# Attention scores of one head and 128 tokens in row halves of TensorE, with q and k transposed on TensorE in float32

## The chip, the cores and the metric

The kernel runs on one core of one Trainium2 chip. The metric is device microseconds of one execution, the median of several; lower is better. Engines are called PE (TensorE matmul), PEld (TensorE weight load), DVE (VectorE), ACT (ScalarE), POOL (GpSimd) and SP (SyncE, which issues most DMAs).

## The reference

Three layers follow each other. The first is causal attention with a decay bias over 4 batches, 8 heads, 576 tokens, head size 64; its rows (2304 x 512) go through a mixture of 8 experts with one expert per token, and then through a dense two-layer net.

```python
scores = scale * np.matmul(q, k.transpose(0, 1, 3, 2))
cum = np.cumsum(np.maximum(s, 0.0), axis=-1)
bias = -(cum[:, :, :, None] - cum[:, :, None, :])
scores = np.where(causal, -1000000000.0, scores + np.minimum(bias, 0.0))
attn = np.exp(scores - np.max(scores, axis=-1, keepdims=True))
attn = attn / (np.sum(attn, axis=-1, keepdims=True) + 1e-09)
x = np.matmul(attn, v)                      # to rows of 8 * 64 = 512
...
ye = np.maximum(xe @ w1[e], 0.0) @ w2[e]    # one expert e per token, gated
...
g = h * np.clip(h + 3.0, 0.0, 6.0) / 6.0    # h = x @ w_in
out = g @ w_out
```

## The kernel before

Every float32 product is made of float16 halves: x = hi + lo, and a product is hi*hi + hi*lo + lo*hi. The change touches the attention stage alone, and the experts and the dense net follow it in program order on the same engines.

Tokens of a batch are cut into blocks i = 0 to 4 of 128 rows (the last has 64), and a block with a pair p of heads is one `Pair`. There are 80 of them: 64 with 128 rows ("full") and 16 with 64 rows ("short"). Block i attends to W = 128 * (i + 1) keys (the short one to 576). For each pair the program writes these steps: `S`, the scores into PSUM (PE); `A`, add the decay sum `cp`, take the minimum and negate (DVE); `E`, the exponential (ACT); `T`, transposes of the weights in float32 (PE, L588); `CD`, the split of the transposed weights into `hi` (ACT, L610) and `lo` (DVE, L611); `V`, the product with v into `o` (PE, L644). `finish` divides by the row sum (DVE, L655 to L657). The steps of neighbouring pairs are interleaved in one loop over slots n: `T` of pair n-1, `S` of pair n+1, `A` and `E` of pair n, `V` of pair n-2. A scheduler of the recording layer then settles each engine's order, and engines execute strictly in that order.

In `S` of the kernel before, rows of the score tile are 64 tokens of each of the two heads, for tokens of one parity r. One matmul of 128 rows times 64 columns (L545) gives hi*hi + hi*lo for one head from a doubled k; one of 64 times 64 (L550) gives lo*hi; a 128 x 128 one adds the causal mask (L556). PSUM holds three score banks (`psS`), two for `o` (`psO`) and three for transposes (`psT`).

q and k come as float32 with tokens in rows. `prep` splits them into halves in row form (POOL L406, L467, L481; for the first 512 tokens of batch 0 on ACT and DVE, L457 to L461), and DMA transposes issued by SP (L440) turn them into `qT` and `kT`. The decay sums are computed for all heads at once, written to DRAM (`cum_d`, L394) and read back by broadcast into `cp` (L401), one head in each half of the partitions. v is loaded by DMA, scaled on ACT (L491), rounded on ACT (L492), and its rest is taken on POOL (L493). When the pieces of `prep` are issued is set by planned times (`at_time`, with a `lag` ahead of their use).

## Time and profile before

| quantity | value |
|---|---|
| median of 3 runs | 906.51 us (905.99 to 907.49) |
| the profiled execution's own time | 901.45 us |
| its span, first to last instruction | 899.8 us |
| mean granted TensorE clock | 0.967 |
| first expert matmul starts (end of attention) | 282.87 us |
| PE busy over the span | 834.1 us (93%) |

The profile shows one execution of the program. A duration of a matmul in it includes the way through the array, so the time that a stream of matmuls takes is read from start to start. "Idle before" an instruction is time in which its engine stood still, put down to what released it.

### The profile page before, as it was taken

The numbers are of one execution on the slowest core, as the hardware profiler recorded it, in microseconds if no ns is written. First come the engines' busy times: TensorE is split into PE (matmuls) and PEld (weight loads), VectorE is DVE, ScalarE is ACT, GpSimd is POOL, SyncE is SP. The second block draws the span as 40 slices with busy tenths as digits, with TensorE's granted clock in tenths as the row PEclk, the third lists the DMA queues.
The fourth block names the chain that finished last, engine by engine and source line by source line (L and its number), as shares of the span: only waits on it lengthen the run. The fifth ranks groups of instructions, "written<-read, shape, count | busy, mean of one in ns | idle before, by whom it ended". The sixth has DMA issues, their size and how long they took to land. (4 is left out here: it accounts for less than half of the span.)

```text
span 899.8 us, 17411 instructions
## 1 busy us (share of the span) xinstructions
PE 834.1 (93%) x6676; PEld 510.6 (57%) x6676; DVE 487.4 (54%) x1250; ACT 428.4 (48%) x831; POOL 260.9 (29%) x357
## 2 busy tenths in 40 slices
PE   2899899989989989899999999999999999999993
PEld 1466565667648987566777744444444444466441
DVE  5477774686856644977869489970351044013000
ACT  3587774699744343665546276640351044023000
POOL 3187869488742212232332100001000100000100
PEclk9999996699979999999999999999999999999997
DMA  8999999943125496988877213310000000000000
GB/s 182 177 209 191 200 211 168 197 147 121 31 55 111 144 210 190 278 308 266 261 217 265 71 48 105 107 48 35 12 1 12 24 12 0 24 24 1 24 36 14
DMA packets 147633, 106.61 MB, mean 118 GB/s; under 512 B 106838, under 2 KB 123478, under 8 KB 147542
## 3 DMA queue, kind: packets, MB, share of 16 engines
q1 hardware_dynamic: 143750, 95.36, 42.0%
q0 software_dynamic: 3792, 10.06, 3.5%
q8 instruction: 54, 0.88, 0.4%
q14 instruction: 37, 0.30, 0.1%
HBM read 78.65 MB, written 9.66 MB: 98 GB/s over the span
## 5 line engine op out<-in xcount | busy, mean ns | idle before, releaser
L1219 PE MATMUL ph<-x2T,wi 128*128 128x512 f16 (+1 forms) x960 | 187.4, 358 | 0.0
L1093 PE MATMUL py<-wo,gT 128*128 128x512 f16 x864 | 187.1, 379 | 0.0
L1219 PEld LDWEIGHTS <-wi 128*128 128x128 f16 x960 | 94.0, 98 | 92.8
L1093 PEld LDWEIGHTS <-gT 128*128 128x128 f16 x864 | 84.5, 98 | 101.7
L1225 DVE SCALAR_TENSOR_TENSOR t<-t,ph 128x512 f32<-128x512 f32 (+1 forms) x80 | 50.5, 632 | 141.3 <-ACT t L1224 141.2
L1260 POOL DMA_INDIRECT out_dram<-o,orows x18 | 17.6, 977 | 355.7 <-ACT o L1258 346.3
L1081 PE MATMUL ph<-xsT,t 128*128 128x224 f16 (+7 forms) x960 | 110.0, 276 | 8.2 <-DVE hT L1086 7.0
L1193 PE MATMUL py<-hT,t 128*128 128x224 f16 (+7 forms) x960 | 109.2, 273 | 6.3 <-DVE hT L1086 5.9
L1081 PEld LDWEIGHTS <-t 128*128 128x128 f16 x960 | 86.9, 100 | 28.9 <-issue 9.1
L1193 PEld LDWEIGHTS <-t 128*128 128x128 f16 x960 | 85.4, 98 | 28.6 <-issue 9.0
L1258 ACT ACTIVATE o<-py 128x512 f32<-128x512 f32 x18 | 10.7, 597 | 163.5 <-PE py L1093 163.5
L611 DVE SCALAR_TENSOR_TENSOR lo<-pt,hi 128x256 f16<-128x256 f32 (+3 forms) x144 | 72.6, 521 | 27.8 <-ACT hi L610 27.0
L610 ACT ACTIVATE hi<-pt 128x256 f16<-128x256 f32 (+3 forms) x144 | 63.8, 461 | 42.3 <-PE pt L588 41.3
L257 DVE SCALAR_TENSOR_TENSOR t<-wf,t 128x1024 f16<-128x1024 f32 x53 | 64.6, 1222 | 34.8 <-ACT t L254 34.5
L575 ACT ACTIVATE pp<-ne,nm 128x128 f32<-128x128 f32 (+4 forms) x144 | 76.9, 581 | 13.2 <-DVE nm L569 13.2
L588 PE MATMUL pt<-idf,pp 128*128 128x128 f32 (+1 forms) x400 | 74.6, 306 | 5.1 <-ACT pp L575 2.6
L569 DVE CUSTOM_DVE_ANT_0 ne<-sp,cp 128x128 f32<-128x128 f32 (+4 forms) x144 | 61.5, 456 | 29.7 <-ACT pp L575 10.9
L254 ACT ACTIVATE t<-wf 128x1024 f16<-128x1024 f32 x53 | 55.6, 1055 | 43.7 <-DMA wf<-in_moe_w_dram 43.4
L1226 ACT ACTIVATE gT<-t 128x512 f16<-128x512 f32 (+1 forms) x80 | 46.9, 586 | 49.8 <-DVE t L1225 49.8
L644 PE MATMUL o<-v,hi 128*128 128x65 f16 (+2 forms) x960 | 64.6, 204 | 5.8 <-ACT hi L610 5.4
L1227 DVE SCALAR_TENSOR_TENSOR gT<-t,gT 128x512 f16<-128x512 f32 (+1 forms) x80 | 51.0, 638 | 31.3 <-ACT gT L1226 29.7
L1224 ACT ACTIVATE t<-ph,three 128x512 f32<-128x512 f32 (+1 forms) x80 | 51.3, 642 | 32.0 <-PE ph L1219 32.0
(170 smaller groups left out, 1097.4 us busy)
## 6 DMA issues: line engine op xcount, KB each, us to landing
wf<-in_moe_w_dram SPq DMA_DIRECT2D x64, 512.0 KB, 6.0
wd<-in_moe_w_in_dram SPq DMA_DIRECT2D x16, 512.0 KB, 5.4
wd<-in_moe_w_out_dram SPq DMA_DIRECT2D x16, 512.0 KB, 3.7
v<-in_v_dram SPq DMA_DIRECT2D x36, 128.0 KB, 4.4
k<-in_k_dram SPq DMA_DIRECT2D x8, 512.0 KB, 5.1
q<-in_q_dram SPq DMA_DIRECT2D x8, 512.0 KB, 5.9
x_d<-xw SPq DMA_DIRECT2D x16, 256.0 KB, 3.3
cp<-cum_d SPq DMA_DIRECT2D x6, 576.0 KB, 7.4
```

Source lines behind the costliest of these rows:

```text
L254: nc.scalar.activation(hi, fv, AF.Copy, scale=sc)
L257: stt(out=lo, in0=fv, scalar=sc, in1=hi, op0=ALU.mult, op1=ALU.subtract)
L569: mark["dve"] = nc.vector.tensor_tensor_reduce(out=ne[:, a:z], in0=sp, in1=c[:, a:z], op0=ALU.add, op1=ALU.min, scale=-1.0 / SC, scalar=se ...
L575: mark["act"] = nc.scalar.activation(self.view(self.pp, e), self.view(self.ne, e), AF.Exp, bias=self.nm[:, e:e + 1], scale=-1.0).ins
L588: nc.tensor.transpose(dst, src, idf)
L610: nc.scalar.activation(hi, pt, AF.Copy, scale=SP)
L611: stt(out=lo, in0=pt, scalar=SP, in1=hi, op0=ALU.mult, op1=ALU.subtract)
L644: mark["pe"] = nc.tensor.matmul(dst, a, x, start=first, stop=last).ins
L1081: mark["pe"] = nc.tensor.matmul(ph[:, :n], wt[c][:, a, cols], xT[:, KD * b_ + c, :n], start=(c == 0 and x == 0), stop=(c == KD - 1 and x = ...
L1093: nc.tensor.matmul(py[:n], hT[i_][:, f, a:a + n], wt[:, j_, f, :], start=(f == 0 and x == 0), stop=(f == nk - 1 and x == 2),)
L1193: nc.tensor.matmul(py[:, :rows], wt2[:, j_, f, cols], hT[i_][:, f, :rows], start=(f == 0 and x == 0), stop=(f == KF - 1 and x == 2),)
L1219: nc.tensor.matmul(ph[:, :n], wi[:, a, kk, fs], x2[:, KD * b_ + kk, :n], start=(kk == 0 and x == 0), stop=(kk == KD - 1 and x == 2),)
```

## The change: what it does

`S` now makes the scores of one head and 128 tokens at a time. The contraction is over 64 rows: head 0 of a pair uses rows 0 to 63 of the array, head 1 rows 64 to 127, and each gets a PSUM bank of its own, so a pair holds a tile of two banks (`psS` has two such tiles, `psO` one bank). The three half products of the two heads alternate, and an explicit order (`ahead`) keeps them so. The causal mask is two more matmuls for each head (`sel` times `mk`, `sel` times `dg`). k is no longer doubled.

q and k are transposed on PE in float32 (`flip`, L469 of the changed kernel) and split after that: `hi` on ACT and `lo` on DVE for k; for q a copy on ACT, and both halves on POOL. Before the transposes POOL copies blocks of 256 tokens into head order (`line_up`). The first 256 tokens of batch 0 skip that copy, since their loads bring them in head order. The decay sums are broadcast to all 128 partitions for each of the 8 heads (`cp` doubles), and `fold_cum` rebuilds the old form for the short blocks on POOL. The scaled copy of v moves from ACT to POOL. The order of the first loads, the `lag`, and some planned times of token routing change.

```diff
-        psS = at.enter_context(tc.tile_pool(name="psS", bufs=3, space=PSUM))
-        psO = at.enter_context(tc.tile_pool(name="psO", bufs=2, space=PSUM))
-
-        kTs, cums, loaded, qTs = {}, {}, {}, {}
+        psS = at.enter_context(tc.tile_pool(name="psS", bufs=2, space=PSUM))
+        psO = at.enter_context(tc.tile_pool(name="psO", bufs=1, space=PSUM))
...
+                if (b, c) == (0, 0):
+                    to = flat.rearrange("p (x r h d) -> x r p h d", x=2, r=2, d=D)
+                    rows = src[b, hs, t0:t0 + n, :].rearrange("h (p r) d -> r p h d", r=2)
+                    for r in range(2):
+                        ld = nc.sync.dma_start(to[hs.start // 4, r], rows[r])
...
+        sel = ac.tile([128, 2, 2, 64], BF16, name="sel")
+        mk = ac.tile([128, 2, 64], BF16, name="mk")
+        dg = ac.tile([128, 64], BF16, name="dg")
+        nc.vector.memset(sel, 0.0)
...
+            for x, r in ((0, 0), (0, 1), (1, 0)):
+                nc.vector.tensor_copy(sel[rows, x, r], idb[rows, rows])
+            nc.vector.tensor_scalar_mul(dg[rows], idb[rows, rows], -1.0e9 * SC)
...
+        def load_cum(b, hs, a=0, z=S):
 
             if b not in cums:
-                cums[b] = a2.tile([128, NP, S], F32, tag="cp", name="cp")
-            rows = cum_d.rearrange("(b p e) t -> b e p t", b=B, e=2)[b, e:e + 1, ps[0]:ps[-1] + 1]
-            return nc.sync.dma_start(
-                cums[b][64 * e:64 * e + 64, ps[0]:ps[-1] + 1], rows.partition_broadcast(64)[:, 0]
-            )
+                cums[b] = a2.tile([128, H, S], F32, tag="cp", name="cp")
+            rows = cum_d.rearrange("(b h o) t -> b o h t", b=B, o=1)[b, :, hs, a:z]
+            return nc.sync.dma_start(cums[b][:, hs, a:z], rows.partition_broadcast(128)[:, 0])
+
+        def fold_cum(b, p):
+
+
+
+            if b not in both:
+                both[b] = cums[b] if b + 1 < B else a2.tile([128, H, S], F32, tag="cp", name="cp")
+            for e in range(2):
+                if e or b + 1 == B:
+                    rows = slice(64 * e, 64 * e + 64)
+                    hi16(both[b][rows, 2 * p], cums[b][rows, 2 * p + e])
...
-            def turn(to, x, ps, a=0, z=n):
-                return nc.sync.dma_start_transpose(
-                    out=to[:, ps].rearrange("p a r f t -> p (a r f) t"),
-                    in_=x[a:z, ps].rearrange("p a r f d -> p (a r f d)"),
-                )
...
+                def line_up():
+                    x = src[:m, w * ps[0]:w * ps[-1] + w]
+                    if big and not fast:
+                        x = a2.tile([128, 512], F32, tag="xs", name="xs", bufs=3)
+                        hi16(
+                            x.rearrange("p (r h d) -> p h r d", r=2, d=D),
+                            x32[kind][:, 2 * ps[0]:2 * ps[-1] + 2].rearrange("p h (r d) -> p h r d", d=D),
+                        )
+                    box.append(x)
...
+                def flip():
+                    x = box.pop()
+                    pk = psT.tile([128, 4, 128], F32, tag="T", name="pk").rearrange("p a t -> p (a t)")
+                    with tc.issue_after(mark["pe"]) if "pe" in mark else ExitStack():
+                        for y in range(len(ps)):
+                            dst = pk[:, n * y:n * y + n]
+                            for r in range(nr):
+                                at = 128 * (len(ps) * r + y)
+                                mark["pe"] = nc.tensor.transpose(
+                                    dst.rearrange("p (j r t) -> p r j t", r=2, t=64)[:, r] if big else dst,
+                                    x[:, at:at + 128], idf[:m, :m],
+                                ).ins
+                    ps_ = slice(ps[0], ps[-1] + 1)
+                    hi, lo = to[:, 0, ps_], to[:, 1, ps_]
+                    x = pk[:, :n * len(ps)].rearrange("p (a t) -> p a t", t=n)
+                    if kind == "k" or fast:
+                        nc.scalar.activation(hi, x, AF.Copy)
+                        stt(out=lo, in0=x, scalar=1.0, in1=hi, op0=ALU.mult, op1=ALU.subtract)
+                        return
+                    xs = a2.tile([128, 512], F32, tag="xs", name="xs", bufs=3)
+                    xs = xs[:, :n * len(ps)].rearrange("p (a t) -> p a t", t=n)
+                    nc.scalar.activation(xs, x, AF.Copy)
+                    hi16(hi, xs)
+                    gtt(out=lo, in0=xs, in1=hi, op=ALU.subtract)
...
-                    nc.scalar.activation(v32[:m], v32[:m], AF.Copy, scale=SV)
-                    nc.scalar.activation(vt[:m, :, 0:D], v32[:m], AF.Copy)
+                    nc.scalar.activation(vt[:m, :, 0:D], v32[:m], AF.Copy, scale=SV)
+                    hi16(v32[:m], v32[:m], SV)
...
-                for (r, a, z), dst in zip(regs, self.sp):
-                    for e, rows in halves:
-                        nc.tensor.matmul(
-                            dst[rows], qT[:, p, r, e, cols], keys(slice(0, 128), e, a, z),
-                            start=True, stop=False,
-                        )
-                    for e, rows in halves:
-                        nc.tensor.matmul(
-                            dst[rows], qT[rows, p, r, e, cols], keys(rows, 2, a, z),
-                            start=False, stop=z < W,
-                        )
-                    if z == W:
-                        m = mk[:, r] if self.full else mk[:, 0, 0]
-                        nc.tensor.matmul(dst[:, 128 * i - a:W - a], idb, m, start=False, stop=True)
+                    self.sp = [bank[:, 0], bank[:, 1, :W - 512]]
+                    work = [[(sp[rows], rows, a, z) for e, rows in halves] for sp, a, z in zip(self.sp, (0, 512), (512, W))]
+                for two in work:
+                    for x, (f, g) in enumerate(((0, 0), (0, 1), (1, 0))):
+                        for dst, rows, a, z in two:
+                            prods.append((dst, qT[rows, f, p, cols], kT[rows, g, p, a:z], x == 0, x == 2 and z < W))
+                    for x in range(2 if self.full else 1):
+                        for dst, rows, a, z in two:
+                            if z == W:
+                                lead, m = sel[rows, x].rearrange("p r t -> p (r t)")[:, :n], mk[rows]
+                                at = 128 * i - a
+                                m = dg[rows] if x else m.rearrange("p r t -> p (r t)")[:, :n]
+                                prods.append((dst[:, at + 64 * x:], lead, m, False, x == 1 or not self.full))
+                ahead = None
+                for dst, lead, m, first, last in prods:
+                    with tc.issue_after(ahead) if ahead else ExitStack():
+                        ahead = nc.tensor.matmul(dst, lead, m, start=first, stop=last).ins
...
-                c = cums[self.b][:, self.p, :self.W]
...
+                c = cums[self.b][:, 2 * self.p + e, :self.W] if self.full else both[self.b][:, 2 * self.p, :self.W]
...
+        some, rest = slice(0, 2), slice(2, H)
+        then(load_cum, 0, some, 0, 256)
+        then(load_cum, 0, rest, 0, 256)
+        then(load_v, 0, 0)
+        then(load, 0, 1)
...
-        lag = 10.0
+        lag = 5.0
...
-            at_time(routed + 6.0, lambda us=us: place_tokens(us))
+            at_time(routed + 8.0, lambda us=us: place_tokens(us))
```

Where the instructions stand now. On PE, at a pair of block 3 of batch 0 (W = 512), `sp` is the score tile, `qT` and `kT` are the transposed halves, `mk` the mask and `idb` an identity. Before, one parity of the pair:

```order
L545 LDWEIGHTS qT
L545 MATMUL sp<-kT,qT 64x512
L545 LDWEIGHTS qT
L545 MATMUL sp<-kT,qT 64x512
L550 LDWEIGHTS qT
L550 MATMUL sp<-kT,qT 64x512
L550 LDWEIGHTS qT
L550 MATMUL sp<-kT,qT 64x512
L556 LDWEIGHTS idb
L556 MATMUL sp<-mk,idb 128x128
L644 LDWEIGHTS hi
L644 MATMUL o<-v_0_189,hi 128x65
```

Now, the end of such a pair, whose six products of 128 x 512 stand in one row (`sel` is a doubled identity, `dg` the diagonal part of the mask, `pk` a transpose of the next block's k):

```order
L554 LDWEIGHTS qT
L554 MATMUL sp<-kT,qT 128x512
L554 LDWEIGHTS sel
L554 MATMUL sp<-mk,sel 128x128
L554 LDWEIGHTS sel
L554 MATMUL sp<-mk,sel 128x128
L554 LDWEIGHTS sel
L554 MATMUL sp<-dg,sel 128x64
L554 LDWEIGHTS sel
L554 MATMUL sp<-dg,sel 128x64
L469 MATMUL pk<-idf,k_240 128x64 x4
```

Eight product matmuls and two masks in three formats of the array (128 x 64, 64 x 64, 128 x 128), once for each parity, became six products and four masks in one format, and float32 transposes of q and k stand between the pairs. In the program's PE order the score matmuls of all pairs form 95 unbroken stretches before and 78 now.

On SP, the start of the program, after the load of s (`cum_d` is the write of the decay sums, `cp` their broadcast, `wgf` the gate weights). Before:

```order
L323 DMA k_151<-in_k_dram 128x8x128
L323 DMA q_150<-in_q_dram 128x8x128
L323 DMA k_155<-in_k_dram 128x8x128
L323 DMA q_154<-in_q_dram 128x8x128
L350 DMA wgf_101<-in_moe_w_gate_dram 128x4x8
L350 DMA wgf_102<-in_moe_w_gate_dram 64x2x8 x4
L394 DMA cum_d<-cum_sb 32x576
L440 DMA_TRANSPOSE kT<-k_219 128x24x64
L440 DMA_TRANSPOSE qT<-q_218 128x16x64
L401 DMA cp<-cum_d 64x576 x2
L401 DMA cp<-cum_d 64x3x576 x2
L333 DMA v_272<-in_v_dram 64x8x64 x2
```

Now:

```order
L327 DMA k_151<-in_k_dram 128x4x64 x2
L327 DMA q_150<-in_q_dram 128x4x64 x2
L327 DMA k_151<-in_k_dram 128x4x64 x2
L327 DMA q_150<-in_q_dram 128x4x64 x2
L403 DMA cum_d<-cum_sb 32x576
L410 DMA cp<-cum_d 128x2x256
L410 DMA cp<-cum_d 128x6x256
L341 DMA v_217<-in_v_dram 64x8x64 x2
L329 DMA k_221<-in_k_dram 128x8x128
L329 DMA q_220<-in_q_dram 128x8x128
```

The write of the decay sums moved ahead of the second block's k and q and of the gate weights, no transpose stands between it and the broadcast, and the broadcast's first part holds 256 of the 576 columns.

## Rows read from the trace of the kernel before

**Rows 1.** Windows: from:to, length, PE PEld DVE ACT POOL busy, PEclk, DMA share, GB/s.

```profile
17.30:41.50 24.20, 21.27 (x129) 10.16 (x129) 8.66 (x45) 9.62 (x26) 1.13 (x1) 1.00 0.98 189
41.50:140.50 99.00, 92.07 (x1182) 62.37 (x1180) 72.72 (x253) 75.14 (x162) 78.14 (x107) 0.98 1.04 202
140.50:171.20 30.70, 30.70 (x280) 18.29 (x279) 14.77 (x67) 14.40 (x37) 21.82 (x27) 0.50 0.94 176
171.20:283.00 111.80, 103.31 (x1366) 71.15 (x1365) 80.62 (x280) 83.85 (x174) 74.91 (x104) 0.95 0.34 91
283.00:512.00 229.00, 214.57 (x1910) 170.77 (x1909) 160.26 (x311) 114.14 (x206) 59.13 (x74) 0.99 0.75 225
```

**Rows 2.** Timeline of PE, a pair with 512 keys: start, length (us), instruction, count.

```profile
61.94 0.41 PE L545 MATMUL sp<-kT,qT 128*64 128x512 f16 x2
62.27 0.40 PE L550 MATMUL sp<-kT,qT 64*64 64x512 f16 x2
62.61 0.23 PE L556 MATMUL sp<-mk,idb 128*128 128x128 bf16 x1
62.77 0.41 PE L545 MATMUL sp<-kT,qTs 128*64 128x512 f16 x2
...
63.44 0.24 PE L644 MATMUL o<-v,hi 128*128 128x65 f16 x2
63.52 0.63 PE L588 MATMUL pt<-idf,pp 128*128 128x128 f32 x4
63.98 0.19 PE L644 MATMUL o<-v,lo 128*128 128x65 f16 x1
```

**Rows 3.** Timeline of PE, a pair with 128 keys.

```profile
135.40 0.25 PE L545 MATMUL sp<-kT,qT 128*64 128x128 f16 x2
135.57 0.24 PE L550 MATMUL sp<-kT,qT 64*64 64x128 f16 x2
135.75 0.23 PE L556 MATMUL sp<-mk,idb 128*128 128x128 bf16 x1
```

**Rows 4.** Groups by line and shape, 40 to 283 us: count | busy, mean ns | idle before.

```profile
L611 DVE SCALAR_TENSOR_TENSOR lo<-pt,hi 128x512 f16<-128x512 f32 x48 | 32.7, 687 | 14.4 <-ACT hi L610 14.1
...
L610 ACT ACTIVATE hi<-pt 128x512 f16<-128x512 f32 x48 | 27.9, 591 | 15.2 <-PE pt L588 14.9
...
L569 DVE CUSTOM_DVE_ANT_0 ne<-sp,cp 128x512 f32<-128x512 f32 x32 | 21.0, 686 | 6.1 <-ACT pp L575 5.1 <-PE sp L556 1.1
...
L657 DVE TENSOR_TENSOR xr<-o,den 128x256 f32<-128x256 f32 x35 | 14.7, 419 | 0.4
...
L406 POOL TENSOR_SCALAR k<-k 128x512 f16<-128x512 f32 x24 | 14.2, 614 | 6.5 <-DMA k<-in_k_dram 6.5
...
L481 POOL TENSOR_TENSOR k<-k,k 128x512 f16<-128x512 f32 x12 | 13.7, 1157 | 0.0
...
L491 ACT ACTIVATE v<-v 128x512 f32<-128x512 f32 x15 | 9.4, 625 | 6.8 <-DMA v<-in_v_dram 6.8
...
L655 DVE TENSOR_SCALAR den<-o 128x4 f32<-128x4 f32 x34 | 5.3, 157 | 7.3 <-PE o L644 7.0
```

**Rows 5.** Timeline of the start, all engines.

```profile
9.92 0.52 SPq L394 DMA_DIRECT2D cum_d<-cum_sb  x1
...
17.29 0.32 PE L545 MATMUL sp<-kT,qT 128*64 128x128 f16 x2 [17.29 <-DMA qT<-q]
...
20.20 0.29 DVE L569 CUSTOM_DVE_ANT_0 ne<-sp,cp 128x128 f32<-128x128 f32 x1 [6.31 <-DMA cp<-cum_d]
...
24.70 0.29 DVE L569 CUSTOM_DVE_ANT_0 ne<-sp,cp 128x128 f32<-128x128 f32 x1 [3.99 <-DMA cp<-cum_d]
```

**Rows 6.** Timeline ahead of the two falls of the clock in 100:141.

```profile
105.44 0.63 ACT L491 ACTIVATE v<-v 128x512 f32<-128x512 f32 x1 [3.00 <-DMA v<-in_v_dram]
...
106.67 0.29 PE L644 MATMUL o<-v,hi 128*128 128x65 f16 x2 [2.28 <-ACT hi L610]
...
137.08 0.63 ACT L491 ACTIVATE v<-v 64x512 f32<-64x512 f32 x1 [3.09 <-DMA v<-in_v_dram]
```

More of the change, by code (lines that the diff above doesn't have):

```diff
@@ L341 @@
         nc.sync.dma_start(s_sb, s.rearrange("b h t -> (b h) t"))
[L342 to L343 removed]
+        load(0, 0, slice(0, H // 2))
+        ahead = [load(0, 0, slice(H // 2, H)).ins]
         wv = w_gate.rearrange("(c r e d) n -> e r d c n", r=2, e=2, d=D)
@@ L347 @@
         ]
-        for to, src in gate_in:
-            with tc.issue_after(ahead[0]):
-                ahead[0] = nc.sync.dma_start(to, src).ins
         def split_gate():
@@ L496, in prep @@
             vs = [v_part(t0 // 128 + j) for j in range(nr)]
-            if fast:
-                return first, vs, (turn_q, turn_k)
-            return [q_part(0), q_part(1)] + [kh_part(0), kh_part(1)] + [kl_part(r) for r in range(nr)] + vs
+            groups = ((0, 1), (2, 3)) if big else (range(NP),)
+            steps = [turn(kind, ps) for ps in groups for kind in "kq"] + [[f] for f in vs]
+            return steps
         class Pair:
@@ L518, in __init__ @@
                 elif i == 0:
-                    self.groups = [[(j, r) for j in js for r in range(2)]]
+                    self.groups = [[(0, e) for e in range(2)]]
                 else:
-                    self.groups = [[(j, r) for j in js] for r in range(2)]
+                    self.groups = [[(j, e) for j in js] for e in range(2)]
                 self.pt = {}
@@ L526, in S @@
                 qT, kT = qTs[self.b, i // 2], kTs[self.b]
-                def keys(rows, f, a, z):
-                    if a == 512:
-                        return kT[1][rows, p, 0, f]
-                    return kT[0][rows, p, :, f, a // 2:z // 2].rearrange("p r (j t) -> p j r t", t=64)
-                bank = lambda: psS.tile([128, 512], F32, tag="S", name="sp")
+                bank = psS.tile([128, 2, 512], F32, tag="S", name="sp")
+                prods = []
                 halves = ((0, slice(0, 64)), (1, slice(64, 128)))
-                q0 = 64 * (i % 2) if self.full else 0
@@ L535, in S @@
-                cols = slice(q0, q0 + 64)
+                q0 = 128 * (i % 2) if self.full else 0
+                cols = slice(q0, q0 + n)
                 if self.full:
-                    one = bank() if 2 * W <= 512 else None
-                    self.sp = [bank()[:, :W] if one is None else one[:, W * r:W * r + W] for r in range(2)]
-                    regs = [(r, 0, W) for r in range(2)]
-                else:
-                    self.sp = [bank(), bank()[:, :W - 512]]
-                    regs = [(0, 0, 512), (0, 512, W)]
@@ new lines, in S @@
+                    work = [[(self.sp[e], rows, 0, W) for e, rows in halves]]
+                else:
+                    self.sp = [bank[:, 0], bank[:, 1, :W - 512]]
[11 more added lines that the diff above has]
+                                prods.append((dst[:, at + 64 * x:], lead, m, False, x == 1 or not self.full))
@@ L945, in fill_tables @@
                 nc.sync.dma_start(row_d.rearrange("(p a) o -> p a o", p=128), none[:, :NROWD // 128])
+        for b in range(B):
+            for p in range(NP):
+                at_unit(NCH * b + (3 if b + 1 < B else 2), p, lambda b=b, p=p: fold_cum(b, p))
         at_slot(4, split_gate)
```

155 lines of the change are left out of this document (50 added, 105 removed).

## The prediction

> **What bounds the kernel now.** I read the windows by stage first, then the timeline of PE inside the attention stage, then the groups of instructions with their waits, and last the start and the places where the granted clock fell.
>
> The windows show where PE is not full [rows 1]. The attention stage ends at 283 us. The expert stage (283 to 512) has PE busy for 214.6 of 229 us, and what follows is PE work too, so whatever the attention stage gains should reach the end. From 41.5 to 140.5 PE is busy for 92 of 99 us, ACT for 75, DVE for 73, POOL for 78, and the DMA engines are full (share 1.04). From 140.5 to 171.2 PE is busy all the time at a granted clock of 0.50, which is the lower of its two levels. PE comes first, but DVE and ACT are not far below it, and that decides how much of a PE saving arrives.
>
> **Scores, the main term.** Start to start, the two L545 matmuls of 512 columns take 0.33 us together, and so do the two L550 ones [rows 2]. With 128 columns they take 0.17 [rows 3]. So 384 columns cost 0.16 us, or 0.42 ns a column, both column halves run side by side, and 0.12 us remains as a fixed part at each group. The mask takes 0.16 us [rows 2], 0.05 of it for its columns. Each group stands in another format of the array than the one before it. Two L644 matmuls with weights of their own, in one format, take only 0.08 us [rows 2], so I put the 0.12 down to the change of format and not to the group.
>
> Before, a full pair has two parities of two groups and a mask: 2 x (2 x (0.12 + W x 0.42 ns) + 0.16) is 1.00, 1.23, 1.44 and 1.64 us for W = 128 to 512. The sum, 5.31, times 16 is 85 us. A short pair (two groups of 512 columns, two of 64, a mask) comes to 1.1 us, 17.6 in all: 102 us.
>
> After, three products over W, masks of 128 and 64 columns, and two changes of format a pair (78 stretches for 80 pairs) give 3 x W x 0.42 ns + 0.08 + 0.24 = 0.48, 0.64, 0.80 and 0.96 us: 2.88 x 16 = 46 us. Short pairs come to 0.99 us each, 16 in all: 62 us. The term is **-40 us**.
>
> The bounds: if each of the five groups of a pair paid 0.12 us, the full pairs would take 69 us and the short ones 25, and the term would be -8. If row halves of 128 columns do not run side by side, the product columns of full pairs count twice, 26 us more, and their masks 5 more, and the term is -9. No row shows such halves. The nearest row is L550, whose two matmuls use different rows and different columns of the array and take 0.33 us together where one alone needs 0.21 + 0.12 [rows 2]. I therefore take -40.
>
> The Trainium skill, page TensorEngine Tiling (Array Packing), section Key Properties, says that a switch of the tiling mode drains TensorE while a switch of tile does not. By that rule the score term is the -40 worked out above, and not -8; the trace agrees with 0.12 us at each switch [rows 2, 3]. The same page, Gotcha 1, speaks against the change: row tiles cannot use one PSUM bank at the same time. By it the heads of a short pair, which share a bank, would run one after the other and 16 pairs would take some 12 us longer, an estimate from the columns above. The trace disagrees already before the change, because the two L550 halves share a bank and take 0.33 us together [rows 2].
>
> **Transposes on PE.** There are 160: 16 in each of 8 blocks of 256 tokens and 8 in each of 4 blocks of 64. Four of L588 take 0.46 us start to start [rows 2], 0.115 each. 128 x 0.115 plus 32 with half the columns at 0.06 give **+17 us**. They stand in the format of their neighbours, so I add no change of format. They wait for POOL's copy in the 28 groups that need one; the copies are issued two units of the plan ahead. POOL's own load stays about even. A later block of 256 tokens cost it six L406 and four of the L481 kind, 8.3 us, and now costs six and two, 6.0 us [rows 4]. The scaled copies of v (20 x 0.61) and the folding of decay sums (20 of about the same length) take that back.
>
> **The other engines.** ACT gets a copy out of PSUM for each group of transposes, 28 x 0.59 and 8 of half the size, 19 us, and loses 20 scaled copies of v at 0.625, 12.5 us: +6.5. DVE gets the `lo` half of k, 14 x 0.687 and 4 halves, +11 us [rows 4]. How much of PE's relief of 40 - 17 = 23 us arrives? For a pair with 512 keys PE now needs 1.64 + 8 x 0.115 + 24 x 0.04 = 3.5 us, and later about 2.8 plus 0.2 for the transposes. DVE needs two of L569, two of L611 and half of `finish` (L655 and L657), 3.0 us [rows 4], and later 0.14 more. So for the wide pairs DVE comes to stand where PE stood, after some 0.3 of 0.7 us. With ACT and DVE as bound I let 10 of the 23 us through: **+13 us** given back (bounds 0 and +23).
>
> **The start.** PE first runs at 17.29 us, when the transposed q lands. DVE's first addition waits until 20.20 for `cp`, and again until 24.70. The write of the decay sums left at 9.92 us [rows 5], behind the gate weights. After, that write comes right behind the first loads, no DMA transpose precedes the broadcast, and the first part is smaller. I expect the first addition at about 14 us: **-6 us** (bounds 0 and -8, since twice the partitions are written).
>
> **The load of v and the clock.** At 105.44 and 137.08 us ACT, which works in order, had stood for 3.0 and 3.1 us at L491 for a late v. PE then had nothing to do for 2.28 us [rows 6], and the second time about as long, and from 140.5 us the granted clock was 0.50 for 30.7 us. At the rate of the 99 us before it (11.9 matmuls a us), its 280 matmuls would have taken 23.5 us, so that stretch cost about 7. The change takes all DMA transposes of q and k off DMA engines that are full there, doubles `cp`, and moves L491 to POOL. I take **-5 us** (bounds -11 and 0, as the clock may fall elsewhere).
>
> **One bank for `o`.** The next group of `V` must now wait until `finish` has read the last one. Its two shown steps take 0.58 us [rows 4], at most 20 us over 35 hand-overs if nothing stood between. The scheduler puts `S` and `T` there: **+4 us** (bounds 0 and +20).
>
> **Sum.** 901.45 - 40 + 17 + 13 - 6 - 5 + 4 = 884.5 us against the profiled execution. The median of the runs was 5.1 us above it, so I forecast 889 us.
>
> **The rivals.**
>
> *Full relief.* ACT and DVE absorb their new work in the idle time that they have (24 and 26 of 99 us [rows 1]), and nothing is given back: 889 - 13 = 876 us. The idle time speaks for it, the 512-key pairs against it.
>
> *Nothing arrives.* The three engines are so close that their hand-overs eat all 23 us, and the start and v alone remain: 899 us, up to 905 with a longer wait for `o`. For it speaks that 48 L611 waited 14 us for ACT, and 48 L610 waited 15 us for PE [rows 4], in a chain that has to pass all three engines; against it, that PE is the one that hardly stood still.
>
> *The clock, the slower side.* A PE that has less work idles more often. The one long stretch at 0.50 followed idle time of 2 to 3 us and cost about 7 us [rows 1, 6]. Three such stretches more than now use up the 17 us that I forecast; with four the time is 917 us. For it speaks that idle times of that length come from waits that the change shifts to POOL and to one bank of `o`; against it, that the shown falls came from the late v.
>
> *Row halves do not run side by side.* The score term is -9, PE gets 8 us more work, nothing is given back to others: 901.45 - 9 + 17 - 6 - 5 + 4 + 5.1 = 907.5 us.
>
> **How the numbers follow.** Forecast 0.43 (own range 880 to 897), full relief 0.25, nothing arrives 0.15, the clock 0.12, no side by side 0.05. The predicted time is 889 us. Leaving out the lower tail of full relief (with a start and a v term at their bounds, 867) and the clock gives 868 to 908 us. A measurement tells about 0.2% from no change. Faster takes the first two cases and two thirds of the third, 0.78; same 0.06; slower 0.16.
>
> **What would show it.** Pairs of score matmuls should start together and 512-key pairs take about 1 us start to start, with 0.12 at both ends; transposes (L469) 0.115 each; the first DVE addition near 14 us; no ACT wait for v; DMA share well below 1 from 41 to 171 us; DVE and ACT above 0.8 busy in the attention stage, which ends near 265 us. The prediction is wrong if score halves start one after another, if PE stands for `xs` copies or for `finish` for more than 10 us in all, or if the clock is at 0.50 for much over 40 us after the start.

## The result, and the profile after

The changed kernel takes 898.79 us (median of 5 runs, 895.72 to 899.82) against 905.99 us before (5 runs beside it). The ratio is 0.9919, with a 95% interval of 0.9893 to 0.9945: 7.2 us faster, where 17 were forecast. The time lies in the range of 868 to 908 us. It meets almost exactly the rival "nothing arrives" (899 us), which had a chance of 0.15; in part that is luck, since this rival also counts a gain from v and the clock that did not come, and the scores gave more than forecast.

The profiled execution of the changed kernel took 895.72 us, 5.7 less than the one before. The first expert matmul starts at 276.39 us. Before it started at 279.46 us; the 282.87 in the table ahead belongs to a later one. So the attention ends 3.1 us earlier, and 2.6 us come after it, where the change touches nothing.

Windows of the changed kernel, with the same cuts as [rows 1] as far as they fit (from:to, length, PE, PEld, DVE, ACT, POOL busy, PEclk, DMA share, GB/s):

```profile
14.50:41.50 27.00, 21.83 (x223) 15.32 (x225) 16.98 (x72) 16.65 (x42) 13.36 (x19) 0.87 0.96 247
41.50:140.50 99.00, 84.43 (x1277) 64.38 (x1272) 73.77 (x253) 73.42 (x157) 64.49 (x92) 0.95 0.51 134
140.50:171.20 30.70, 28.25 (x437) 20.88 (x430) 26.71 (x105) 26.04 (x65) 21.72 (x38) 1.00 0.38 121
171.20:276.40 105.20, 87.36 (x1177) 65.81 (x1178) 67.33 (x229) 72.98 (x147) 80.44 (x107) 0.82 0.34 93
```

Against [rows 1], the long stretch at the lower clock from 140.5 us is gone, and up to 171.2 us the DMA share is halved. PE is no longer full anywhere, and the last 105 us have a granted clock of 0.82 where 0.95 stood. No other engine is full over any of these long stretches either.

The scores came as forecast. PE's timeline of the changed kernel, a full pair with 512 keys, a short pair, and a full pair with 128 keys (start, length, instruction, count):

```profile
162.00 0.82 PE L554 MATMUL sp<-kT,qT 64*128 64x512 f16 x6
162.64 0.23 PE L554 MATMUL sp<-mk,sel 64*128 64x128 bf16 x2
162.70 0.21 PE L554 MATMUL sp<-dg,sel 64*128 64x64 bf16 x2
162.84 0.55 PE L582 MATMUL pt<-idf,pp 128*128 128x128 f32 x3
...
66.17 0.93 PE L554 MATMUL sp<-kT,qTs 64*64 64x512 f16 x12
66.93 0.20 PE L554 MATMUL sp<-mk,sel 64*64 64x64 bf16 x2
67.06 0.24 PE L637 MATMUL o<-v,hi 128*128 128x65 f16 x2
67.14 1.07 PE L469 MATMUL pk<-idf,xs 128*128 128x128 f32 x8
68.04 0.19 PE L637 MATMUL o<-v,lo 128*128 128x65 f16 x1
...
131.51 0.34 PE L554 MATMUL sp<-kT,qT 64*128 64x128 f16 x6
131.69 0.22 PE L554 MATMUL sp<-mk,sel 64*128 64x128 bf16 x2
131.74 0.19 PE L554 MATMUL sp<-dg,sel 64*128 64x64 bf16 x2
131.86 1.09 PE L582 MATMUL pt<-idf,pp 128*128 128x128 f32 x8
```

Six products of 512 columns take 0.64 us, that is 0.21 for each two, so row halves run side by side. A pair takes 0.84 us with 512 keys and 0.35 with 128, a little under the 0.96 and 0.48 of the forecast. Eight transposes take 0.90 us, 0.113 each. The heads of a short pair share a PSUM bank, and their twelve products take 0.76 us: they run side by side too. The Trainium skill, page TensorEngine Tiling (Array Packing), Gotcha 1, says that row tiles cannot use one bank at the same time; the 12 us that this would have cost by the forecast's estimate aren't there.

The start came too (compare [rows 5]): the decay sums leave at 7.62 us, and the first additions run at 14.53 and 17.03 us.

```profile
7.62 0.33 SPq L403 DMA_DIRECT2D cum_d<-cum_sb  x1
...
14.53 0.29 DVE L567 CUSTOM_DVE_ANT_0 ne<-sp,cp 128x128 f32<-128x128 f32 x1 [5.07 <-DMA cp<-cum_d]
...
17.03 0.29 DVE L567 CUSTOM_DVE_ANT_0 ne<-sp,cp 128x128 f32<-128x128 f32 x1 [1.38 <-DMA cp<-cum_d]
```

Where it went shows when PE's time is added up by step. The table has the time from each PE instruction's start to the next one's in the attention, waits included; it is worked out from the records of the two traces.

| step (count before, after) | before, us | after, us |
|---|---|---|
| scores (784, 864) | 113.8 | 68.1 |
| transposes of q and k (0, 160) | 0 | 30.1 |
| T (400) | 66.3 | 77.6 |
| V (1440) | 57.8 | 75.9 |

The scores gave 45.7 us. Of the 30.1 us of the new transposes, 10.2 belong to the first 16, ahead of the first addition, and 5.3 of these are idle time; the other 144 take 19.9. T and V, which have the same work as before, take 29.4 us more, and 24.0 of that is recorded idle time behind them: PE waits. By the windows of both kernels PE's idle time in the attention rose from 18.3 us (from 17.3 us on) to 40.0 (from 14.5 us on), and the time at the lower clock from 44.4 to 54.6 us, now in eight stretches of 3.4 to 14 us.

Progress shows at what time it was lost. The time at which the n-th of 160 score maxima is ready:

| n | 0 | 32 | 64 | 88 | 104 | 112 | 128 | 136 | 144 | 159 |
|---|---|---|---|---|---|---|---|---|---|---|
| before, us | 20.4 | 66.5 | 111.8 | 158.0 | 182.0 | 195.8 | 222.7 | 230.8 | 240.6 | 269.0 |
| after, us | 14.7 | 62.2 | 103.5 | 147.5 | 165.8 | 185.2 | 214.2 | 223.5 | 241.9 | 265.9 |

The changed kernel is 16 us ahead at n = 104 and 3 at the last. The lead is lost between n = 104 and 144, where the changed kernel has 30.7 us at the lower clock and the kernel before has none. The largest step is 8.6 us between n = 136 and 144, of which 4.4 are made up by the last. The windows of this step, first of the kernel before, then of the changed one:

```profile
230.90:240.70 9.80, 9.80 (x125) 6.47 (x124) 8.55 (x37) 7.26 (x20) 5.12 (x11) 1.00 0.12 35
223.60:241.90 18.30, 15.12 (x162) 10.92 (x159) 10.00 (x40) 17.37 (x35) 17.28 (x23) 0.72 0.52 173
```

ACT and POOL are nearly full there in the changed kernel; 8.4 us of ACT's 17.4 are the preparation of expert weights (L244, L245, L250), which no experiment took away.

Groups of the changed kernel from 40 to 276 us (compare [rows 4]), and its longest kinds of wait there:

```profile
L604 DVE SCALAR_TENSOR_TENSOR lo<-pt,hi 128x512 f16<-128x512 f32 x48 | 32.4, 685 | 10.4 <-ACT hi L603 9.8 <-issue 0.4
...
L603 ACT ACTIVATE hi<-pt 128x512 f16<-128x512 f32 x48 | 27.8, 595 | 10.7 <-PE pt L582 10.1 <-remote 0.3 <-issue 0.2
...
L424 POOL TENSOR_SCALAR cp<-cp 64x576 f32<-64x576 f32 x20 | 13.4, 671 | 10.0 <-DMA tok_d<-what,pos_s 6.2 <-ACT xw L666 2.7
...
L493 ACT ACTIVATE v<-v 128x512 f16<-128x512 f32 x13 | 8.0, 632 | 3.4 <-DMA v<-in_v_dram 3.4
```

```profile
PE sp L554 <- DVE nm L567: 6.7, 13, 0.9
PE sp L554 <- POOL qTs L424: 5.4, 2, 3.2
PE o L637 <- issue: 4.7, 6, 2.0
```

The second view has us in total, times, and the longest one. ACT's wait for v is 3.4 us here, half of what stood in [rows 4]. PE's waits are small ones for many engines. The longest, 3.2 us, stands at the end of a batch: the short block's q halves (`qTs`) come late from POOL. POOL, DVE and PE at the end of batch 2:

```profile
179.24 1.31 POOL L424 TENSOR_SCALAR cp<-cp 64x576 f32<-64x576 f32 x2 [3.88 <-DMA tok_d<-what,pos_s]
180.64 0.62 POOL L424 TENSOR_SCALAR xs<-k 128x512 f32<-128x512 f32 x1
181.22 0.62 POOL L424 TENSOR_SCALAR xs<-q 128x512 f32<-128x512 f32 x1
181.80 0.41 POOL L424 TENSOR_SCALAR qTs<-xs 128x256 f16<-128x256 f32 x1
...
182.27 2.50 PE L554 MATMUL sp<-kT,qTs 64*64 64x512 f16 x16 [2.28 <-POOL qTs L424]
...
185.00 0.23 DVE L567 CUSTOM_DVE_ANT_0 ne<-sp,cp 128x64 f32<-128x64 f32 x1 [4.15 <-POOL wf L249]
185.15 0.42 DVE L650 TENSOR_TENSOR xr<-o,den 128x256 f32<-128x256 f32 x1
```

`fold_cum` (L424 on `cp`) writes where block 3's `A` still reads, so by the program it waits for DVE's `A` of block 3, one of which ended at 178.88 us; it stood until 179.24. The DMA named as releaser isn't what held it: with the fold on DVE (below), POOL went on at 173.97 us, right behind its last `tok_d`. Behind it in POOL's queue stood `qTs`. PE waited 2.28 us for `qTs`, DVE 4.15, and the granted clock was 0.50 (the 1.2 GHz level) from 173.3 to 187.0 us; it fell during an earlier idle time of PE (2.00 us, up to 174.00), ahead of the wait for `qTs`. The end of batch 1 looks the same (118.55 us: PE waited 3.16).

### The profile page after: what moved, and what is told of

Same layout as the page of the kernel before. It is cut to its first block, busy times and chain, and to the rows that moved or that the text cites. A ratio compares the mean times of both kernels' runs of the same rounds, so it can differ in the third digit from the quotient of the medians.

```text
span 894.0 us, 17932 instructions
## 1 busy us (share of the span) xinstructions
PE 818.4 (92%) x6916; PEld 521.0 (58%) x6916; DVE 493.2 (55%) x1257; ACT 433.6 (48%) x835; POOL 262.4 (29%) x369
## 4 chain that ended last, share of the span: by engine, by line
issue 43%; PE 9%; DMA 8%; DVE 4%; POOL 3%; SPq 2%; ACT 2%; POOLq 0%; DVEq 0%; ACTq 0%
PE py L1186 5%; DMA wf<-in_moe_w_dram 5%; PE ph L1074 4%; POOL out_dram L1253 2%; DMA xg<-x_d,slots 1%; DVE t L257 1%; ACT t L254 1%; SPq L215 1%; DMA xsT<-xg 1%; SPq L239 1%; DMA wd<-in_moe_w_in_dram 1%; DMA slots<-tok_d 1%; DVE hT L1079 0%; DVE m L1051 0%; DVE wi L1054 0%
## 5 line engine op out<-in xcount | busy, mean ns | idle before, releaser
L582 PE MATMUL pt<-idf,pp 128*128 128x128 f32 (+1 forms) x400 | 77.6, 310 | 9.0 <-DVE kT L478 2.2
```

The source lines that it names most:

```text
L582: nc.tensor.transpose(self.pt[g][:m, x, :], src, idf)
```

## The experiments

The theories: A, PE's work sets the attention's end. C, POOL's queue at the batch ends paces it. D, the one bank of `o` does. E, what PE gives up is taken by waits in the loop over three engines. F, the loss is one of instruction order. Ratios are to the kernel before on the same chip; medians of the kernel before lay between 900.9 and 911.0 us from chip to chip, so ratios of different groups are compared with care. The letters differ in two of the texts below: A in that of pe_twice_after stands for what is E here, and A1 to A3 are guesses at single causes. Except where the order is said to be held, an edit also brings a new order of the instructions on every engine (in before_one_o_bank 219 of DVE's 1250 stand at another place), and its ratio has both.

**More work for PE.** T's transposes were done twice for head pairs 0 and 1, 200 more transposes, 22 us:

```
+ for _ in range(2 if self.p < 2 else 1):
      nc.tensor.transpose(...)                 # in T
```

> The kernel before, with the 200 transposes T of head pairs 0 and 1 made twice (the second overwrites the first with the same values). At 0.11 us each this is 22 us more of PE work and no work for any other engine. Theory A (the kernel before was bound by PE in the attention stage): 16 to 24 us slower, 922 to 930 us. Rival (it was already bound by the hand-overs between engines): 0 to 10 us slower.

> The changed kernel with the same edit: 22 us more of PE work. Theory A (PE is no longer the bound, the saving on scores was lost in waits on other engines): 4 to 12 us slower than the changed kernel, 903 to 911 us. Rival B (PE still is the bound, and a lower granted clock took the saving): 18 to 26 us slower, 917 to 925 us.

Before: 1.0067 [1.0036, 1.0098], 6 us. After: 1.0161 [1.0119, 1.0204], 22 us over the changed kernel. Before the change, then, 22 us of PE's work cost 6: PE was busy, but less than a third of that work reached the end. A part of the rest is the clock's. In the profile the stretches at the lower clock shrank from 44.4 to 20.5 us as PE had more to do, and the median of the mean granted clocks was 0.985 against 0.966 for the kernel before. Among the executions of the kernel before, in five groups of 17 to 32, a mean clock higher by 0.01 went with 3.2 to 3.9 us less time (6.0 in a sixth group of ten). By this the clock gave back some 6 to 7 us, an estimate. That the same edit costs 22 us in the changed kernel is what "PE still is the bound" had said. It is no proof of that, since T stands inside the loop and the order is new; the held order below tells more.

**Banks of PSUM.**

```
- psS bufs=2 (tiles of two banks)   + psS bufs=3 (single banks)     three_score_banks
- psO bufs=1                        + psO bufs=2                    three_score_banks
- psT bufs=3, psO bufs=1            + psT bufs=2, psO bufs=2        o_two_banks
- psO bufs=2                        + psO bufs=1                    before_one_o_bank
```

> The changed kernel with two PSUM banks for o, and two in place of three for transposes (8 banks in all). Theory A1 (V waits for finish because o has one bank): 5 to 10 us faster than the changed kernel, 889 to 894 us. Rival A2 (the third transpose bank was needed as much, or the wait for o is hidden): 897 to 910 us.

> The changed kernel with the PSUM banks of the kernel before: three single banks for scores (in place of two pairs) and two for the sums o (in place of one). Theory D, that one bank for o costs what the hand-overs show (15 of 35 in which the next V starts 0.14 us after finish, 1 to 4 us each of stall on TensorE): 4 to 15 us back, a ratio of 0.975 to 0.988, if three single banks serve the scores as well as two pairs. Rival, that the scores miss the fourth bank: the next pair's scores can start only when both A of the pair before it have read theirs, about 1 us for each of 140 pairs on the path; ratio 1.00 to 1.05. If neither binds, 0.99.

> The kernel before with one bank for the sums o in place of two, and nothing else. Theory D: one bank costs 4 us (0 to 20 as the forecast put it), a ratio of 1.002 to 1.02, with V's waits for finish in the trace. Rival: V of a block's next half comes more than 2 us behind finish anyway, and the ratio is 1.000, within 0.2%.

Measured: 1.0656 [1.0614, 1.0698], 0.9912 [0.9885, 0.9940] and 0.9987 [0.9958, 1.0017]. The plan of banks of before inside the changed kernel changes nothing, and neither does one bank of `o` in the kernel before: nothing speaks for D, though both have a new order. The third bank for transposes is another matter; without it the kernel is by the ratios some 66 us slower than the changed one, more than any new order cost here.

**Work off POOL.**

```
- if kind == "k" or fast:             + if True:                              q_split_on_dve
- if kind == "k" or fast:             + if kind == "k" or fast or not big:    short_q_on_dve
- hi16(both[..], cums[..])            + nc.scalar.activation(both[..], cums[..], AF.Copy)   fold_on_act
```

> The changed kernel with q split like k, hi on ACT and lo on DVE straight out of PSUM, without the copy on ACT and the two halves on POOL: POOL loses 25 us, DVE gains 11 us, ACT about the same. Theory A3 (late q halves from POOL hold PE up, 5.4 us of idle time and two falls of the clock): 4 to 8 us faster, 891 to 895 us. Rival (DVE is the tight engine): 898 to 906 us.

> The changed kernel, with the q halves of the short block alone split by ScalarE and VectorE, as k is. GpSimd's fold is left where it is but nothing of the scores stands behind it any more. Theory C (the fold in GpSimd's queue holds up the short block's scores, 6 to 12 us): the ratio is 0.979 to 0.987, the 3 us waits for qTs at the batch ends gone. Rival (the chain bound by ScalarE and VectorE): ScalarE and VectorE change by under 1 us a batch, and the ratio stays at 0.99.

> The changed kernel, with the copies of fold_cum (64x576, 0.67 us each on GpSimd) made by ScalarE. Theory C: GpSimd works in order, and the fold, which must wait until VectorE's A of block 3 has read the decay sums, stands ahead of the short block's q halves; the waits behind it (about 3 us of TensorE and 4 us of VectorE at the end of each of the first three batches, and the low clock after them) cost 6 to 12 us. Then this kernel is at a ratio of 0.979 to 0.986 to the kernel before (882 to 889 us against 906), and the waits for qTs at about 118 and 182 us are gone. Rival, that these waits only show where a chain bound by ScalarE and VectorE stands still: ScalarE has 12 us more work, and the ratio stays at 0.99 to 1.00. With theory A (TensorE's work decides) nothing changes either: 0.99.

Measured: 1.0049 [1.0021, 1.0077], 0.9949 [0.9906, 0.9992] and 1.0006 [0.9972, 1.0040]. None is faster than the changed kernel. By these runs C would fall. But each edit had moved more than its own lines, as the next group showed.

**Work left out.** The scores without their third product (computation changed: q's high by k's low half), and V with `lo` replaced by `hi` for head pairs 0 and 1 (72 `lo` instructions of DVE left out):

```
- for x, (f, g) in enumerate(((0, 0), (0, 1), (1, 0))):   + enumerate(((0, 0), (1, 0)))    fewer_scores_after
- for e, rows in halves: matmul(.., keys(rows, 2, a, z))  (left out)                       fewer_scores_before
+ if self.p > 1: stt(out=lo, ...)                                                          no_lo
- lh, ll = self.lhs(e, j)             + lh, ll = ... if p > 1 else (lh, lh)                no_lo
```

> The kernel before with the third product of the scores (q's high half by k's low half, two of the four matmuls of a register of scores) left out: about 45 us less of TensorE's work in the attention, as much as the change takes off, and no transposes, no other bank plan and nothing on other engines. Theory A (TensorE's work sets the attention's end, and what the change lost it lost by its own additions): the time falls by 30 to 45 us, ratio 0.950 to 0.967. Theory E (the loop of S, A, E, T, copy, lo and V runs over three engines of which ScalarE and VectorE are already 80% busy, and they hold what TensorE gives up): the time falls by 5 to 15 us, ratio 0.983 to 0.995, TensorE's gaps go from 18 to over 40 us and the stretches at the low clock grow.

> The changed kernel with one of the three products of the scores left out: about 17 to 20 us less of TensorE's work. Theory A: the time falls by 15 to 20 us, to a ratio of 0.970 to 0.976 to the kernel before. Theory E: by 0 to 6 us, ratio 0.985 to 0.992, and TensorE's gaps grow by about what was left out.

> The kernel before with VectorE's low halves of the weights left out for head pairs 0 and 1 (72 instructions of about 0.53 us, 38 us of VectorE); TensorE's V multiplies the high half twice in their place, so its work is the same. Theory A (TensorE bounds the attention before): the time falls by under 8 us, ratio over 0.991. Theory E with VectorE in the loop: 10 to 25 us, ratio 0.972 to 0.989.

> The changed kernel with the same low halves left out. Theory E (TensorE's relief was taken up by VectorE and ScalarE): the time falls by 15 to 30 us, a ratio of 0.959 to 0.975 to the kernel before, more than the same edit gives in the kernel before. Theory A, or the clock alone: under 8 us, ratio over 0.983.

Measured: 0.9966 [0.9932, 1.0000], 1.0175 [1.0119, 1.0231], 0.9911 [0.9876, 0.9945] and 1.0073 [1.0038, 1.0108]. Two kernels with less work were slower than the changed one, by 23 and 14 us. No theory said so. The order of the instructions suggested a reason: a scheduler draws it up for each engine at build time, and every edit makes it draw up another. In the trace of fewer_scores_after, 243 of DVE's 1257 instructions and 114 of POOL's 369 stand at another place than in the changed kernel's.

**The same with the order held.** The four kernels again, with an edge from each instruction to the next one of its engine, so that those left stand in the order of the kernel they were taken from (in the trace of fewer_scores_after_same_order 2 of DVE's and none of POOL's stand elsewhere):

```
+ for names in recorded_order.values():        # one list per engine
+     for one, two in zip(names, names[1:]):
+         tc.add_manual_dep(traced[two], one, ...NoSync...)
```

> The kernel before without the third product of the scores, as in fewer_scores_before, but with the instructions that remain issued on every engine in the very order of the kernel before (there they stood differently at 65 to 865 places of an engine). Theory E (what TensorE gives up is taken by waits for ScalarE and VectorE, whatever the order): the time falls by 3 to 10 us, ratio 0.988 to 0.997, TensorE's gaps over 40 us. Theory F (the gain was lost to the new order that the scheduler drew up for the edited kernel): the time falls by 25 to 45 us, ratio 0.95 to 0.972.

> The changed kernel without one of the three products of the scores, issued in the very order of the changed kernel. Theory F (the 23 us that fewer_scores_after lost were the new order's): the ratio to the kernel before is 0.972 to 0.993, no slower than the changed kernel, and the attention ends before 277 us. Theory E with the low clock (less work on TensorE makes its clock fall, and the falls cost more than the work): as in fewer_scores_after, ratio 1.00 to 1.02, low clock in the attention over 75 us.

> The kernel before without the same low halves, issued in the very order of the kernel before. Theory E: VectorE is in the loop before too, the time falls by 5 to 12 us as in no_lo_before (ratio 0.987 to 0.995), less than the same edit in the changed kernel in its own order. If the order made no_lo_before's 8 us: ratio 0.997 to 1.000.

> The changed kernel without the low halves of head pairs 0 and 1 (38 us less of VectorE), issued in the very order of the changed kernel. Theory E (VectorE holds TensorE in the changed kernel): the time falls by 12 to 30 us below the changed kernel's, ratio 0.96 to 0.98. Theory F alone (only the order matters, VectorE isn't the holder): 0 to 6 us, ratio 0.985 to 0.993. If the ratio is again over 1.00, both fall.

| order held | ratio, interval | attention ends, us | new order, ratio |
|---|---|---|---|
| fewer scores, before | 0.9800 [0.9759, 0.9840] | 273.5 (279.5) | 0.9966 |
| fewer scores, after | 0.9945 [0.9916, 0.9975] | 276.6 (276.4) | 1.0175 |
| no lo, before | 0.9978 [0.9945, 1.0011] | 288.0 (279.5) | 0.9911 |
| no lo, after | 0.9853 [0.9813, 0.9893] | 276.5 (276.4) | 1.0073 |

The attention's end is that of one execution each; in brackets the end in the profile of the kernel that the order is from, taken in another series. Ends of different series don't compare: the kernel before had a median of 911.0 us beside these four runs, and 906.0 beside the changed kernel, where its profiled execution took 901.45. So the ratios decide. Windows of fewer_scores_before_same_order, which correspond to [rows 1], then of no_lo_after_same_order:

```profile
41.50:140.50 99.00, 81.54 (x1036) 58.60 (x1034) 70.66 (x250) 74.17 (x159) 77.92 (x107) 0.90 1.06 203
140.50:171.20 30.70, 28.53 (x297) 18.70 (x297) 17.29 (x72) 17.59 (x45) 23.02 (x29) 0.59 0.95 176
171.20:273.50 102.30, 88.70 (x1137) 63.52 (x1136) 74.60 (x262) 78.51 (x162) 70.74 (x100) 0.87 0.39 93
```

```profile
41.50:140.50 99.00, 84.42 (x1282) 64.89 (x1282) 61.92 (x224) 73.32 (x158) 63.95 (x92) 0.95 0.53 136
140.50:171.20 30.70, 28.13 (x440) 20.95 (x434) 23.12 (x95) 25.36 (x64) 22.32 (x39) 1.00 0.36 113
171.20:276.50 105.30, 86.09 (x1158) 64.05 (x1159) 54.46 (x201) 72.44 (x147) 79.20 (x106) 0.82 0.34 93
```

In the kernel before, 46.1 us of PE's time (the L550 matmuls) went away. PE's other steps took 38 us more in their place (masks 22.4 to 32.0, the other products 45.3 to 53.6, T 66.3 to 75.8, V 57.8 to 68.5), 22 of it recorded idle time behind them, and the time at the lower clock grew from 44.4 to 71.7 us. By the medians the kernel gained 18 us. So some two fifths of the relief arrives, between what E and F had said. In the changed kernel, 9.5 us off the scores gain nothing (0.9945 against 0.9919). About 38 us off DVE gain some 6 us by the ratios (0.9853 against 0.9919, with intervals that just meet), where 12 to 30 were said for DVE as the holder. DVE is at 54 of 105 us there. The profiles of both show the progress of the changed kernel's within about 2 us all the way (n = 112: 184.6, 185.2 and 185.2 us), but on a chip where the kernel before is 5 us slower. A falls for the changed kernel, and so does the reading that DVE's load alone holds it. E stands in its general form: waits take most of the relief, and the lower clock a part; which engine holds the loop is not shown. F is right in part, since the same edit with a new and with the held order differs by 1.7 to 2.3% for three of these four, more than the whole change brought.

**The fold, with the order held.** `fold_cum`'s copies on DVE, and then only those of the first three batches:

```
- hi16(both[..], cums[..])    + nc.vector.tensor_copy(both[..], cums[..])                              all
- hi16(both[..], cums[..])    + (hi16 if b + 1 == B else nc.vector.tensor_copy)(both[..], cums[..])    three
```

> The changed kernel with the copies of fold_cum made by VectorE in place of GpSimd, each behind the A that reads what it overwrites; every other instruction stands in the changed kernel's order (in fold_on_act the scheduler had moved the rest as well). Theory C (the fold in GpSimd's queue, which waits for block 3's A, and the short block's q halves behind it set the pace at the end of each of the first three batches; neither TensorE's nor VectorE's work does): the 3 us waits for qTs go, the attention ends 5 to 10 us earlier (266 to 272 us) and the ratio to the kernel before is 0.980 to 0.987, although VectorE has 20 copies of 0.35 to 0.7 us more. Rival (the pace at the batch ends is set by other links of the same loop, and the wait moves to the next one): the attention ends at 274 to 279 us, ratio 0.990 to 0.997.

> As fold_on_dve_same_order, but only the 12 copies of the first three batches are VectorE's; the 8 of the last batch, which stood together in VectorE's queue there (198.46 to 205.4 us, one of them 2.28 us), stay on GpSimd. All else in the changed kernel's order. Theory C: the 5.6 us by which fold_on_dve_same_order was ahead at 180 us stay, the attention ends at 268 to 273 us, ratio 0.984 to 0.991, faster than the changed kernel. Rival (the pace moves to the next link, as the order was drawn up for the fold on GpSimd): what is won at 180 us is lost again in the last batch, the attention ends at 274 to 278 us, ratio 0.991 to 0.996.

All folds: 1.0017 [0.9987, 1.0047]. The maxima are 5.6 us ahead at n = 112 (179.6 us) and 5.4 behind at the end. The eight copies of the last batch stand together in DVE's queue there; DVE and POOL of fold_on_dve_same_order:

```profile
198.46 4.11 DVE L421 COPY cp<-cp 64x576 f32<-64x576 f32 x3
203.02 2.33 DVE L421 COPY cp<-cp 64x576 f32<-64x576 f32 x5
```

```profile
197.05 2.14 POOL L251 TENSOR_TENSOR t<-wf,t 128x1024 f16<-128x1024 f32 x1
199.15 0.83 POOL L424 TENSOR_SCALAR xs<-k 128x512 f32<-128x512 f32 x1
199.94 2.32 POOL L251 TENSOR_TENSOR t<-wf,t 128x1024 f16<-128x1024 f32 x1
```

Three batches: 0.9866 [0.9821, 0.9911], attention until 273.65 us, 2.7 earlier than the changed kernel, and 11 us under the kernel before by the medians (896.37 against 907.15). It beats the kernel before; against the changed kernel the intervals overlap; the ratios say 5 us, the profiles 2.9. At the end of batch 2 of this kernel, the same places as above:

```profile
178.77 0.40 POOL L424 TENSOR_SCALAR qTs<-xs 128x256 f16<-128x256 f32 x1 [3.56 <-ACT xs L482]
...
180.73 1.36 PE L554 MATMUL sp<-kT,qTs 64*64 64x512 f16 x16
...
182.27 0.23 DVE L567 CUSTOM_DVE_ANT_0 ne<-sp,cp 128x64 f32<-128x64 f32 x1
```

`qTs` comes 3.0 us earlier, PE has no wait ahead of the short block, and DVE's addition runs 2.7 us earlier, which is what the attention's end gained. In fold_on_dve_same_order, with the same copies up to there, `qTs` came still earlier (176.22 us), and the lead at n = 112 was 5.6 us. So C holds at its place, with a price of some 3 to 6 us in two executions and not the 6 to 12 first put on it. That fold_on_act and short_q_on_dve don't show it may be due to their new orders; they weren't run with the order held.

## Why the prediction was right in direction and wrong in size

**Scores, -40; transposes, +17; start, -6: right in kind and near in size.** 45.7 us of start-to-start time came off the scores, and row halves run side by side. A transpose takes 0.113 us at the full clock; the 144 behind the first addition took 19.9 us with their waits. The first addition is 5.7 us earlier. It was right to put the 0.12 us down to the change of format, and not to each group.

**The step that failed: "With ACT and DVE as bound I let 10 of the 23 us through: +13".** From the first addition to the end of the attention the forecast had 11 us of gain (-40 + 17 + 13 - 5 + 4); the profiles show 2.6 us of loss (5.7 ahead at the start, 3.1 at the end). Nothing of PE's relief arrived, so this term comes out at its upper bound of +23, as what is left over when the other terms are read off. In its place stands idle time of PE, 18.3 us before and 40.0 after. The reason given for the term, DVE's load on wide pairs, was wrong too or a small part of it: with the order held, 38 us less of DVE gained some 6 us. What is left is the reading that PE, ACT, DVE and POOL wait for each other in turn, each in its own order and none of them full over the long windows. The runs narrow the loss down to this, but only the wait at `qTs` is shown by taking it away. PE being "first" in the windows was read as PE setting the end. In the kernel before, PE was busy for 92 of 99 us, and yet 46 us off its work gained 18 us, and 22 us on top of it cost 6.

**v and the clock, -5.** The waits for v were halved (6.8 to 3.4 us in the shown group) where none were to be left, the DMA share fell, and the long stretch at the lower clock is gone. But the changed kernel has eight shorter ones, 54.6 us in all against 44.4. So one of the prediction's own signs of being wrong came, the clock at 0.50 for much over 40 us. At the price of the long stretch (7 us for 30.7) that is about +2 in place of -5. The executions of the kernel before give a like price: 3.2 to 3.9 us for 0.01 of the mean clock are 5.4 to 6.6 us for 30.7 us at 0.50. So the rival of the clock, with 7 us for each of three or more further stretches, isn't what happened. This is partly the same loss as the one above, since falls stand beside PE's waits (115.3 and 173.3 us); the runs don't part the two.

**One bank for `o`, +4: no price seen**, in either kernel. In the terms of the forecast the three differences are 10 + 7 - 4 = 13 us, about the 13.6 us (11 and 2.6) that are missing. That is no check, as the first of them is what is left over; and the 5.7 us that the scores gave beyond the forecast were lost too.

**"POOL's own load stays about even".** True of its busy time (181 us up to the end of the attention before, 183 after), but the load was costed and not the queue: a `fold_cum` that waits for DVE stands ahead of `qTs`. That was some 3 to 6 us.

**Left open.** What else paces the changed kernel: ACT and POOL, nearly full for 18 us of the last batch, were not relieved with the order held (but for POOL's fold), and DVE's `lo` still waits for ACT's `hi`. How much of the 7.2 us is due to the new order itself: the change can't be made without one.

## What to carry to other kernels

An engine that is 93% busy needn't set the end: before a saving on it is booked, add work to it or take some away with everything else held, and see what share reaches the end. Where a build step orders the instructions, hold the order when a single edit is to be measured, or the edit and a new order are measured together; here the order alone was worth up to 2.3%, three times the change. When work moves to an engine that works in order, cost the queue and not only the load: ask what the moved instruction waits for, and what stands behind it.

## What the runs showed of the hardware that I had not expected

Less work on PE went with more time at the lower clock, and more work with less: 71.7 us at 0.50 in the attention with fewer scores (order held), 44.4 in the kernel before, 20.5 with T's transposes doubled. These are single executions, and four kernels with the same PE work lay between 24.2 and 58.0 us. The medians of the mean clock agree, each against the kernel before beside it: 0.953 against 0.960 with fewer scores, 0.985 against 0.966 with the doubled transposes. The clock so takes back part of what PE is relieved of, by the estimate above 2 to 3 us of the 46.

A copy of 64 x 576 on DVE took 0.46 us with POOL quiet. At 198.46 us, with POOL at work, three took 4.11 us together, one of them 2.28 us, and ended 0.3 us after POOL's L251. The Trainium skill, page SBUF — State Buffer, section Who interferes with whom, says that such a copy can use a pair of ports that VectorE shares with GpSimd, and that the later of the two stands until the other's instruction has ended; the rows agree.
